# Moving row-reversed filter copies out of the head of a spectral-filter + FFN kernel, with a reordered table build

## Chip, cores, metric

One core of a Trainium2 chip. The metric is device time in microseconds (us). In the lines of profiles PE is TensorE, PEld its weight loads, DVE VectorE, ACT ScalarE, POOL GpSimd, and SPq SyncE issuing DMAs; L12 is a line of that kernel, `a<-b` writes a from b, and a bracket or a second `<-` names what ended a wait.

## The reference, cut

```python
g = sigmoid((x * gate_w).sum(-1, keepdims=True))
a = irfft2(rfft2(x) * (w_r + 1j * w_i))                    # S = 2048, D = 576
b = (gelu(B_x @ w_gate) * (B_x @ w_up)) @ w_down           # F = 4608
out = g * a + (1 - g) * b
# outputs: out and its vjp for x, w_r, w_i, w_gate, w_up, w_down, gate_w; bf16 inputs
```

## The kernel before

A *head* makes Fourier tables by rotation and runs the forward FFT of x; its tiles are stored to DRAM (`scr_x`). Then comes the FFN: 18 groups of 256 columns, four steps each. Every step starts with the z matmuls (L341), which need the group's transposed weights `wdT`. The remaining FFTs and the elementwise "mid" stage of the filter run as side work between the FFN's matmuls. A last phase is pure matmul. What the change touches:

```python
# u2(t), second FFT stage of tile t: evacuate from PSUM, store at once on SyncE's queue (LD)
    V.tensor_copy(Vt[:], vps[:, :, :2 * HF])                 # L538
    ...                                                      # or ScalarE, L540, for some tiles
    LD.dma_start(dst[t], Vt[:])                              # L541
...
# weights of group g, on the same queue, in three parts after steps 0, 1, 2 of group g - 1
    LD.dma_start_transpose(wts[g][1][:, 4:5, :], ...)        # part 1, L241
    LD.dma_start_transpose(wtmp[0][:], B_w_down[fsl, 0:512]) #         L242
    LD.dma_start(wdT[LO, 4, :], wdT[HI, 4, :])               # part 2, L245
    ... LD.dma_start(wdT[r, 2*par:2*par+2, :], wtmp[0][...]) # four moves, L248
...
# row-reversed copies, DRAM to DRAM: 32 of 2 x 128 x 72 elements (36 KB, one row fewer in two), 2 small
def reversed_rows(eng, src, dst):
    s_, d_ = (a.rearrange("(m i) (h l) -> h i m l", i=T, h=2) for a in (src, dst))
    return [lambda i=i: eng.dma_start(d_[:, i], s_[:, T - i, ::-1]) for i in range(1, T)] + ...
...
# head
for t in range(T):
    x1[t]()                                   # first FFT stage
    ...
    if t % 3 == 0 and t + 3 < T:
        build_R(nc, tb, unit, t + 3)          # rotation tables of three tiles
    if t > 0:
        x2[t - 1]()                           # second FFT stage
tail_table()                                  # odd inverse table
for k, v in enumerate((A_w_r, A_w_i)):        # filter copies on GpSimd's queue, all in the head
    for move in reversed_rows(nc.gpsimd, v[:, HF:DF], wrev[k][:]):
        move()
...
# FFN step
def side_work():
    for _ in range(3):                        # products of the mid stage, on VectorE
        if side: side.pop(0)()
...
for _ in range(3):                            # reversed output copies, on SyncE's queue
    if moves: moves.pop(0)()
```

`unit` buffers (tables, FFT tiles, products) share one pool of 19 slots. In the built program SyncE's queue is in order, and its DMAs use eight semaphores in turn, so each waits for the one eight places ahead of it.

Of the kernel before, what the change touches and what calls it, by code (L numbers as in the profile page):

```python
# [11 lines left out]
BF16 = mybir.dt.bfloat16  # L12
# [7 lines left out]
S, D, DF = 2048, 576, 289  # L20
P, T = 128, 16
# [19 lines left out]
HF = 145  # L41
# [60 lines left out]
def run_late(tb):  # L102
    while tb.late:
        tb.late.pop(0)()
# [32 lines left out]
def build_R(nc, tb, unit, t0):  # L137

    V = nc.vector
    n = min(3, T - t0)  # L140
    step = 2.0 * math.pi / S * EPS_SCALE
    X = unit([n, P], I32, name="XR")
    C = unit([n, P], I32, name="CR")
    for t in range(n):
        V.tensor_scalar(X[:, t, :], tb.krow[:], tb.scol[:, t0 + t:t0 + t + 1], None, op0=ALU.mult)
    V.tensor_scalar(C[:], X[:], float(S // 4), None, op0=ALU.add)
    V.tensor_single_scalar(X[:], X[:], S - 1, op=ALU.bitwise_and)
    V.tensor_single_scalar(C[:], C[:], S - 1, op=ALU.bitwise_and)
    o = unit([n, 3, P], name="Rt")

    for v, (ang, b, sc) in enumerate(((C, tb.pi, -step), (X, tb.npi, step), (X, tb.pi, -step))):
        tb.late.append(lambda v=v, ang=ang, b=b, sc=sc: nc.scalar.activation(o[:, :, v, :], ang[:], ACT.Sin, bias=b[:], scale=sc))
    tb.Rt += [o[:, t] for t in range(n)]
# [32 lines left out]
def kernel(  # L186
# [4 lines left out]
    nc = tc.nc  # L191
    LD = nc.sync
# [6 lines left out]
    unit = Unit(ctx.enter_context(tc.tile_pool(name="unit", bufs=NUNIT, side="right")))  # L199
# [12 lines left out]
    wrev, orev = ([dram.tile([S, DF - HF], BF16, name=f"{n}{k}") for k in range(2)] for n in ("wrev", "orev"))  # L212
# [40 lines left out]
    tb = iotas(nc, res, unit)  # L253
# [20 lines left out]
    pz = ps1.enter_context(tc.tile_pool(name="pz", bufs=1, space=PSUM))  # L274
# [16 lines left out]
    def headps():  # L291
        hctr[0] += 1
        pool, tag = ((pg, "pg"), (ph, "xy"), (pz, "z"), (ph, "xy"))[hctr[0] % 4]
        return pool, tag
# [90 lines left out]
    stores, moves = [], []  # L385
# [159 lines left out]
    def tail_table():  # L545

        n = HF - P
        nc.gpsimd.memset(tb.At2[:], 0.0)
        pool, tag = headps()
        tp_ = pool.tile([P, 2, 1024], BF16, tag=tag, name="tp")  # L550
        for c in range(2):
            nc.tensor.transpose(tp_[:, c, 0:P], tb.Dt[2][:, c, 0:P], ident[:])
            nc.tensor.transpose(tp_[0:n, c, 256:256 + P], tb.Dt[2][:, c, P:HF], ident[:])
            nc.tensor.transpose(tp_[:, c, 512:512 + 32], tb.Dt[3][0:32, c, 0:P], ident[0:32, 0:32])
            nc.tensor.transpose(tp_[0:n, c, 768:768 + 32], tb.Dt[3][0:32, c, P:HF], ident[0:32, 0:32])
        V.tensor_copy(tb.Oi[:, :, 0:P], tp_[:, :, 0:P])
        V.tensor_copy(tb.Oi[:, :, P:HF], tp_[:, :, 512:512 + n])
        ot = unit([2, HF], name="ot")
        V.tensor_copy(ot[0:n, :, 0:P], tp_[0:n, :, 256:256 + P])
        V.tensor_copy(ot[0:n, :, P:HF], tp_[0:n, :, 768:768 + n])  # L560
        for i in range(2):
            LD.dma_start(tb.At2[i * NL:i * NL + n, i, :, 0:HF], tb.Dt[1][0:n])
            LD.dma_start(tb.At2[i * NL + n:(i + 1) * NL, i, :, HF:2 * HF], ot[0:n])
# [17 lines left out]
    def tiles_of(t):  # L581
        return t[:].rearrange("(m i) l -> m i l", i=T)

    def reversed_rows(eng, src, dst):

        s_, d_ = (a.rearrange("(m i) (h l) -> h i m l", i=T, h=2) for a in (src, dst))
        return [lambda i=i: eng.dma_start(d_[:, i], s_[:, T - i, ::-1]) for i in range(1, T)] + \
            [lambda: eng.dma_start(d_[:, 0, 1:P], s_[:, 0, P - 1:0:-1]), lambda: eng.dma_start(dst[0:1], src[0:1])]

    a_dv = a_scr[:].rearrange("(m i) d -> m i d", i=T)  # L590
    dxa_dv = dxa_scr[:].rearrange("(m i) d -> m i d", i=T)
# [1 line left out]
    def mid_units():  # L593
# [36 lines left out]
        def products(p):  # L630
            X, G, W = st[p, "x"], st[p, "g"], st[p, "w"]
            i0 = 2 * p

            def halve(t):
                e = t[:].rearrange("p i c l -> p (i c) l")[:, :, 0:DF:DF - 1]
                V.tensor_scalar(e, e, 0.5, None, op0=ALU.mult)

            def bc(ap):
                return ap.unsqueeze(2).to_broadcast([P, 2, 2, DF])

            def mul(key, a, b):
                def f():
                    st[p, key] = unit([2, 2, DF], name=key)
                    V.tensor_tensor(st[p, key][:], a[:], bc(b), op=ALU.mult)
                return f

            def comb(k1, k2, conj):
                def f():
                    m1, m2 = st[p, k1], st[p, k2]
                    V.tensor_tensor(m1[:, :, 0, :], m1[:, :, 0, :], m2[:, :, 1, :], op=(ALU.add if conj else ALU.subtract))  # L650
                    V.tensor_tensor(m1[:, :, 1, :], m1[:, :, 1, :], m2[:, :, 0, :], op=(ALU.subtract if conj else ALU.add))
                return f

            def fold(key):

                def f():
                    m = st[p, key]
                    q = unit([2, 2, 2, HF], name="q" + key)
                    for e, op in enumerate((ALU.add, ALU.subtract)):
                        V.tensor_tensor(q[:, :, :, e, 0:HF - 1], m[:, :, :, 0:HF - 1], m[:, :, :, DF - 1:HF - 1:-1], op=op)  # L660
                    V.tensor_copy(q[:, :, :, :, HF - 1], m[:, :, :, HF - 1:HF].to_broadcast([P, 2, 2, 2]))
                    st[p, key + "_q"] = q
                return f

            def out_dw():
                o = st[p, "o1"]
                nc.gpsimd.tensor_scalar(o[:, :, 1, HF:DF], o[:, :, 1, HF:DF], -1.0, None, op0=ALU.mult)

                def store():
                    for k, v in enumerate((o2v, o3v)):  # L670
                        LD.dma_start(v[:, i0:i0 + 2, 0:HF], o[:, :, k, 0:HF])
                        LD.dma_start(tiles_of(orev[k])[:, i0:i0 + 2, :], o[:, :, k, HF:DF])
                    if p == T // 2 - 1:
                        for k, v in enumerate((out_2, out_3)):
                            moves.extend(reversed_rows(LD, orev[k][:], v[:, HF:DF]))
                stores.append(store)
            return [
                lambda: halve(G),
                mul("m1", X, W[:, 0]), mul("m2", X, W[:, 1]), comb("m1", "m2", False),
                lambda: (halve(st[p, "m1"]), fold("m1")()),  # L680
                mul("n1", G, W[:, 0]), mul("n2", G, W[:, 1]), lambda: (comb("n1", "n2", True)(), fold("n1")()),
                mul("o1", G, X[:, :, 0, :]), mul("o2", G, X[:, :, 1, :]), comb("o1", "o2", True),
                out_dw,
            ]
# [24 lines left out]
        out = [first] + [gap] * 3  # L709
# [92 lines left out]
    x1, x2 = fwd_units(xT, scr_x, None, ps=head_tile)  # L802
    build_R(nc, tb, unit, 0)
    run_late(tb)
    for t in range(T):
        x1[t]()
        if t % 4 == 2 and t < 14:
            tchunk(xn, xT, t + 2)
        if t >= 9 and t % 2 == 1:
            tchunk(dB, dOT, 2 * (t - 9))  # L810
        if t % 3 == 0 and t + 3 < T:
            build_R(nc, tb, unit, t + 3)
        if tb.late:
            tb.late.pop(0)()
        if t > 0:
            x2[t - 1]()
    build_B(nc, tb, unit, res)
    run_late(tb)
    tail_table()
    for k, v in enumerate((A_w_r, A_w_i)):  # L820
        for move in reversed_rows(nc.gpsimd, v[:, HF:DF], wrev[k][:]):
            move()
    x2[T - 1]()
    gate()

    fg = zipped(*fwd_units(dOT, scr_g, gs32))
    ia, pa = inv_units(scr_p1, a_dv, SD2)
    ib, pb = inv_units(scr_p2, dxa_dv, 1.0)
    mid = mid_units()
    fft = fg + [gap] * 5 + mid[:-2] + pa + mid[-2:] + [gap] * 2 + ia[:-4] + pb + ia[-4:] + ib  # L830

    fft_pos = [0]

# [49 lines left out]
    for g in range(NG):  # L883
# [3 lines left out]
        for m in range(NPR):  # L887
            pr = g * NPR + m
# [3 lines left out]
            hs = [h for u in pend[m] for h in u] if pend else []  # L892

            def side_work():
                for _ in range(3):
                    if side:
                        side.pop(0)()
            if g == 0 and m > 0:
                fft_next()
            z, xy_full = H_mm(g, m)  # L900
# [31 lines left out]
            else:  # L932
                jobs = [(0, sig0)] * bool(carry) + carry + [(1.7, second)] + [(0, sig0)] * (not carry) + hs
                us = sum(j[0] for j in jobs)
                at, k, late = 0.0, 1, [sig1]
# [18 lines left out]
                LD.dma_start(gwb[:], gate_w.partition_broadcast(P))  # L954
            if (g, m) in ((0, 3), (1, 0)):
                scale_dB(T // 2)
            for _ in range(3):
                if moves:
                    moves.pop(0)()
            if done[0] == n_slots or (pr >= wgT_from and pr % 2 == 0 and len(wgT_all) < 20):  # L960
                load_wgT()
                if done[0] == n_slots:
                    load_wgT()
# [232 lines left out]
```

## Time and profile before

| | median us | profiled span | mean granted clock | first z matmul |
|---|---|---|---|---|
| before (4 runs, 1489.52 to 1492.24) | 1490.91 | 1494.7 | 0.979 | 87.10 |

TensorE is the bound. Of the 80 us in which it idles, most lie ahead of the first z matmul: 29.2 in one wait. From there on an untouched group takes 52.0 us in the stretch that matters later (its z matmuls start at 394.58, 446.58, 498.63, 550.63). A start of a group's first z matmul is therefore a milestone that can be compared between kernels; I use that as a ledger below. The prediction shows the lines.

### The profile page before, as it was taken

To read this page: it belongs to the slowest core of one execution; us is meant where nothing else is said; L and a number is where in the kernel's file an instruction comes from. 1 tells how busy PE (TensorE), PEld (TensorE's weight loads), DVE (VectorE), ACT (ScalarE), POOL (GpSimd) and SP (SyncE) were. 2 spreads that over 40 slices of the span, in tenths; PEclk is the share of its full clock that TensorE was granted. 3 is DMA by queue.
4 is the path that set the end of the run, shared out by engine and by line. 5 is a ranking of instruction groups with operands and counts; after the bars stand their busy time and mean duration, and the time that the engine had idled before them with its cause. 6 is when DMAs were issued, how large, how long until landed. Compare 5 with 4: busy or idle time off the path is not lost.

```text
span 1494.7 us, 30032 instructions
## 1 busy us (share of the span) xinstructions
PE 1414.5 (95%) x11500; PEld 1050.8 (70%) x11586; DVE 887.8 (59%) x2356; ACT 697.2 (47%) x1380; POOL 172.1 (12%) x258
## 2 busy tenths in 40 slices
PE   4388999999999999998999999999999999999997
PEld 3255767767776776776677777777877777777775
DVE  6269777988898889867677777775000461212200
ACT  3267766666667767666667667664000000000000
POOL 6500011111111111111010010010000110000000
PEclk8699999999999999999999999999999999999998
DMA  9925454455565555446556546665999998878773
GB/s 167 75 76 132 118 147 128 122 136 129 137 155 128 132 141 135 114 103 144 139 133 160 143 127 154 161 143 138 274 199 194 209 213 159 167 158 170 153 150 67
DMA packets 550712, 217.87 MB, mean 146 GB/s; under 512 B 375368, under 2 KB 540424, under 8 KB 550568
## 3 DMA queue, kind: packets, MB, share of 16 engines
q1 hardware_dynamic: 537800, 194.03, 59.4%
q0 software_dynamic: 10960, 20.91, 6.0%
q8 instruction: 90, 1.47, 0.5%
q10 hardware_dynamic: 1808, 1.02, 0.2%
q14 instruction: 54, 0.44, 0.1%
HBM read 43.28 MB, written 96.22 MB: 93 GB/s over the span
## 4 chain that ended last, share of the span: by engine, by line
PE 77%; DVE 2%; issue 1%; DMA 0%; SPq 0%; ACT 0%; DVEq 0%
PE acc L1043 28%; PE wps L464 14%; PE xy L353 12%; PE wps L447 8%; PE z L341 7%; PE wps L477 2%; PE xy L348 2%; PE z L344 1%; PE pf L745 1%; PE pf L772 1%; PE pf L774 1%; DMA pin<-scr 0%; PE pf L695 0%; PE pf L696 0%; PE pf L698 0%
## 5 line engine op out<-in xcount | busy, mean ns | idle before, releaser
L1043 PEld LDWEIGHTS <-pin 128*128 128x128 bf16 x3456 | 338.0, 98 | 86.5 <-DMA pin<-scr 1.4
L353 PE MATMUL xy<-wgu,xT 128*128 128x512 bf16 x1066 | 257.9, 380 | 10.1 <-issue 8.3
L464 PEld LDWEIGHTS <-xn 128*128 128x128 bf16 x2304 | 225.1, 98 | 31.3 <-issue 0.2
L353 PEld LDWEIGHTS <-xT 128*128 128x128 bf16 x1152 | 106.9, 98 | 139.0 <-issue 31.8
L366 ACT ACTIVATE da<-z,omg 128x256 bf16<-128x256 f32 x288 | 113.3, 474 | 126.6 <-PE z L344 123.2
L1060 ACT COPY bo<-acc 128x288 f32<-128x288 f32 x32 | 12.8, 399 | 309.3 <-PE acc L1043 284.7
L447 PE MATMUL wps<-dB,A 128*128 128x288 bf16 x1152 | 152.7, 286 | 0.0
L341 PE MATMUL z<-wdT,dOT 128*128 128x256 bf16 x1152 | 141.1, 277 | 7.0 <-DMA wdT<-wtmp 4.4
L1043 PE MATMUL acc<-wd_all,pin 128*128 128x288 bf16 x1152 | 142.8, 286 | 1.1 <-DMA pin<-scr 1.1
L1043 PE MATMUL acc<-wgT,pin 128*128 128x288 bf16 x1152 | 143.6, 286 | 0.0
L1043 PE MATMUL acc<-wuT,pin 128*128 128x288 bf16 x1152 | 143.6, 286 | 0.0
L447 PEld LDWEIGHTS <-A 128*128 128x128 bf16 x1152 | 112.6, 98 | 34.9
L464 PE MATMUL wps<-dHg,xn 128*128 128x256 bf16 x1152 | 133.1, 273 | 0.0
L464 PE MATMUL wps<-dHu,xn 128*128 128x256 bf16 x1152 | 132.0, 273 | 0.0
L341 PEld LDWEIGHTS <-dOT 128*128 128x128 bf16 x1152 | 112.5, 99 | 26.2 <-issue 6.5
L1120 DVE SCALAR_TENSOR_TENSOR f32t<-gwf,dlog,b16t 128x576 f32<-128x576 f32 x16 | 13.1, 817 | 179.2 <-DMA b16t<-dxa_scr 179.2
L372 ACT ACTIVATE q<-xy 128x512 bf16<-128x512 f32 x144 | 86.1, 598 | 66.0 <-PE xy L353 62.3
L396 ACT ACTIVATE om<-s 128x512 bf16<-128x512 bf16 x144 | 92.0, 639 | 23.7 <-DVE s L380 23.6
L470 POOL DMA_DIRECT2D out_dram<-dw x67 | 48.9, 730 | 440.7 <-ACT dw L425 290.6
L397 ACT ACTIVATE s<-s 128x512 bf16<-128x512 bf16 x144 | 90.7, 630 | 4.6
L378 ACT CAST hu<-xy 128x512 bf16<-128x512 f32 x144 | 87.0, 604 | 0.0
L379 DVE TENSOR_SCALAR s<-q 128x512 bf16<-128x512 bf16 x144 | 41.9, 291 | 73.2 <-ACT q L372 72.5
(213 smaller groups left out, 1846.8 us busy)
## 6 DMA issues: line engine op xcount, KB each, us to landing
scr<-A SPq DMA_DIRECT2D x144, 128.0 KB
scr<-dHg SPq DMA_DIRECT2D x144, 128.0 KB
scr<-dHu SPq DMA_DIRECT2D x144, 128.0 KB
out_dram<-dw POOLq DMA_DIRECT2D x67, 128.0 KB, 2.9
wd_all<-in_B_w_down_dram SPq DMA_DIRECT2D x3, 1728.0 KB
out_dram<-dwd POOLq DMA_DIRECT2D x34, 144.0 KB, 3.2
wgu<-in_B_w_gate_dram SPq DMA_DIRECT2D x18, 256.0 KB
wgu<-in_B_w_up_dram SPq DMA_DIRECT2D x18, 256.0 KB
```

The source lines that it names most:

```text
L341: nc.tensor.matmul(zo(t), lhsT=dOT[:, ci, t, :], rhs=wdT[:, ci, :], start=(t % 4 < 2 and ci == 0), stop=False)
L353: nc.tensor.matmul(xy[k][:, t % 2, :], lhsT=xT[:, ci, t, :], rhs=wgu[:, ci, :], start=False, stop=(ci == 3))
L366: nc.scalar.activation(da[:, tt, :], z[:, tt, k, :], ACT.Copy, scale=omg32[:, t:t + 1])
L372: nc.scalar.activation(q[:], xy[:, :, 0:FG], ACT.Square)
L378: nc.scalar.copy(hu[:], xy[:, :, FG:2 * FG])
L379: V.tensor_scalar(s[:], q[:], A_GELU, 1.0, op0=ALU.mult, op1=ALU.add)
L396: nc.scalar.activation(om[:], s[:], ACT.Sigmoid, scale=-2.0 * C_GELU)
L397: nc.scalar.activation(s[:], s[:], ACT.Sigmoid, scale=2.0 * C_GELU)
L447: nc.tensor.matmul(wps[:, :288], lhsT=tl(0, t)[:, fch * P:(fch + 1) * P], rhs=dB[:, t, h * 288:(h + 1) * 288], start=(t == 0), stop=(t == ...
L464: nc.tensor.matmul(wps[:, cc, :], lhsT=xn[:, t, (c0 + cc) * P:(c0 + cc + 1) * P], rhs=tl(k, t), start=(t == 0), stop=(t == T - 1))
L470: wst[0].dma_start(ov[:, c0:c0 + TPB, fsl], dw[:])
L1043: nc.tensor.matmul(acc[:, :288], lhsT=src[:, r, :], rhs=w_of(r)[:, h * 288:(h + 1) * 288], start=(first and r == 0), stop=(last and r == F ...
```

## The change

Its intent: take the 34 filter copies out of the head, where they share the DMA engines with the loads and stores that hold the FFT up; give the table build and the second FFT stage a tile of slack; spread the copies over the first two groups; make the output copies as soon as each row pair is done.

```diff
@@ tail_table
-        pool, tag = headps()
-        tp_ = pool.tile([P, 2, 1024], BF16, tag=tag, name="tp")
+        tp_ = pz.tile([P, 2, 1024], BF16, tag="z", name="tp")
@@ reversed_rows: the same copies, all on SyncE's queue, for the tiles asked for
-    def reversed_rows(eng, src, dst):
+    def reversed_rows(src, dst, tiles):
...
@@ out_dw, store
-                    if p == T // 2 - 1:
-                        for k, v in enumerate((out_2, out_3)):
-                            moves.extend(reversed_rows(LD, orev[k][:], v[:, HF:DF]))
+                        moves.extend(reversed_rows(orev[k][:], (out_2, out_3)[k][:, HF:DF], [(T - i) % T for i in (i0, i0 + 1)]))
@@ head
-        if t % 3 == 0 and t + 3 < T:
-            build_R(nc, tb, unit, t + 3)
+        if t % 3 == 1 and t + 2 < T:
+            build_R(nc, tb, unit, t + 2)
...
-        if t > 0:
-            x2[t - 1]()
+        if t > 1:
+            x2[t - 2]()
+    x2[T - 2]()
...
-    tail_table()
-    for k, v in enumerate((A_w_r, A_w_i)):
-        for move in reversed_rows(nc.gpsimd, v[:, HF:DF], wrev[k][:]):
-            move()
+    for i in range(T):
+        for k, v in enumerate((A_w_r, A_w_i)):
+            moves.extend(reversed_rows(v[:, HF:DF], wrev[k][:], [i]))
...
-    fft = fg + [gap] * 5 + mid[:-2] + ...
+    fft = fg + [tail_table] + [gap] * 4 + mid[:-2] + ...
@@ FFN step
-                for _ in range(3):
+                for _ in range(4):
                     if side:
...
-            for _ in range(3):
+            for _ in range(5 if pr < 8 else 2):
                 if moves:
                     moves.pop(0)()
+            assert pr != 8 or not moves
```

More of the change, by code (lines that the diff above doesn't have):

```diff
@@ L582, in tiles_of @@
         return t[:].rearrange("(m i) l -> m i l", i=T)
-    def reversed_rows(eng, src, dst):
+    def reversed_rows(src, dst, tiles):
         s_, d_ = (a.rearrange("(m i) (h l) -> h i m l", i=T, h=2) for a in (src, dst))
-        return [lambda i=i: eng.dma_start(d_[:, i], s_[:, T - i, ::-1]) for i in range(1, T)] + \
-            [lambda: eng.dma_start(d_[:, 0, 1:P], s_[:, 0, P - 1:0:-1]), lambda: eng.dma_start(dst[0:1], src[0:1])]
+        out = []
+        for i in tiles:
+            if i:
+                out.append(lambda i=i: LD.dma_start(d_[:, i], s_[:, T - i, ::-1]))
+            else:
+                out.append(lambda: LD.dma_start(d_[:, 0, 1:P], s_[:, 0, P - 1:0:-1]))
+                out.append(lambda: LD.dma_start(dst[0:1], src[0:1]))
+        return out
     a_dv = a_scr[:].rearrange("(m i) d -> m i d", i=T)
@@ L829 @@
     mid = mid_units()
-    fft = fg + [gap] * 5 + mid[:-2] + pa + mid[-2:] + [gap] * 2 + ia[:-4] + pb + ia[-4:] + ib
+    fft = fg + [tail_table] + [gap] * 4 + mid[:-2] + pa + mid[-2:] + [gap] * 2 + ia[:-4] + pb + ia[-4:] + ib
     fft_pos = [0]
```

## The prediction

> **What bounds the kernel now.** I read the page first. TensorE is busy 95% of the span, and its row of 40 slices says where it is not: slices 1 to 3 (37 us each) hold nearly all the gap, and the granted clock falls there too.
>
> ```profile
> PE 1414.5 (95%) x11500; PEld 1050.8 (70%) x11586; DVE 887.8 (59%) x2356; ACT 697.2 (47%) x1380; POOL 172.1 (12%) x258
> ...
> PE   4388999999999999998999999999999999999997
> ...
> PEclk8699999999999999999999999999999999999998
> ```
>
> Idle TensorE time is 1494.7 - 1414.5 = 80 us. From 93 us on almost every microsecond is matmul, so a microsecond saved ahead of the first FFN matmul (87.10) is a microsecond of the total, unless something later makes TensorE wait anew. The waits of the first 140 us name the big one:
>
> ```profile
> PE fx L530 <- ACT Y L519: 35.7, 4, 29.2
> ...
> ACT Rt L152 <- DMA scr_x<-Vt: 28.1, 1, 28.1
> ```
>
> TensorE waits 29.2 us for a copy on ScalarE, which stands behind a rotation table (Rt), which waits for a *store* of a forward-FFT tile (Vt to scr_x). A table need not wait for a store in its data; both live in the same 19-slot pool, so it waits for the slot. The timeline of SyncE's queue tells why that store is late:
>
> ```profile
> 19.97 3.62 SPq L241 DMA_TRANSPOSE wdT<-in_B_w_down_dram  x1
> 23.64 4.16 SPq L242 DMA_TRANSPOSE wtmp<-in_B_w_down_dram  x1
> 34.24 0.50 SPq L245 DMA_DIRECT2D wdT<-wdT  x1
> 39.25 6.83 SPq L248 DMA_DIRECT2D wdT<-wtmp  x4
> 46.18 37.20 SPq L541 DMA_DIRECT2D scr_x<-Vt  x15
> ```
>
> The first Vt was ready at 16.4, but its store is behind the loads of the first weights, whose last moves wait for the DMA transposes (6.4 and 4.4 us of waiting on that queue). It is issued at 46.18 and lands about 55.5. Meanwhile GpSimd's queue runs the row-reversed filter copies (wrev), from 8 to 70 us:
>
> ```profile
> 8.45 7.81 POOL L587 DMA_DIRECT2D wrev<-in_A_w_r_dram  x7
> ...
> 68.86 1.61 POOL L588 DMA_DIRECT2D wrev<-in_A_w_i_dram  x2 [1.45 <-issue]
> ```
>
> In 25 to 45 us the software queue holds 10 to 75% of the 16 engines' time while the whole core moves only 32 to 56 GB/s. The transposes, issued at 20 to 28, have landed at 39. In a later group the same transposes, issued at 530.1 and 531.3, have landed before 537.5, when the moves behind them go out without waiting.
>
> **What the Trainium skill says.** "DMA: Bandwidth & Descriptors", section "Issuing engines are not separate DMA queues": DMAs of all issuing engines run on the same 16 DMA engines and interleave. The trace agrees: GpSimd's copies slow SyncE's transposes. The same page, "Why a DMA increments its semaphore by 16 and not by 1", says that a hardware-issued DMA uses the largest count up to 16 that divides the slowest dimension of both patterns. A reversed copy is 2 x 128 x 72, so 2 engines. The trace agrees: while the existing reversed output copies run alone on SyncE's queue (about 711 to 713) the DMA share is 0.1 to 0.2 at 16 to 28 GB/s. "TensorE: Matmul & The Clock Gate", "What's actually happening", says the array falls to half clock after an idle window of about 3.4 us. The trace agrees: granted clock 0.50 in 40 to 60 us, and 0.75 in 710 to 720 after a wait of 3.81.
>
> **The change part by part.**
>
> *Removed from the head:* 34 wrev DMAs on GpSimd. Without them I estimate the weights: the x and grad loads end near 17 as before; the 1280 rows of the two first weight slices took about 8 us beside the copies and take 4 to 5 later in the trace, so 21 to 22; the transposes need 5 to 6 us as at 530, so 27; the four moves 2.65 us as later in the trace, so about 30; the first scr_x store lands near 32.
>
> *Rotation angles one tile later, second FFT stage two tiles behind:* in the built program the first slot wait on a scr_x store is now on VectorE's angles for tiles 9 to 11, made after tile 7, and ScalarE's first on a store is the copy of tile 9 instead of the table before tile 7. Tile 7 ran at 28.7, so VectorE gets there at about 28 and waits to 32. So the TensorE gap shrinks from 29.2 to about 4.5: **-24.5 us**. The two later waits of ScalarE for scr_x stores (3.9 us together) should mostly go, as the queue is no longer behind: **-3**. Without the long idle, the half-clock restart after 58.8 is mostly saved: **-1.5**.
>
> *The odd table:* 8 small transposes, 1.07 us of TensorE at 82.0 to 83.1, move into the FFN loop (slot 33, about step 8). TensorE is the bound there too: **0**.
>
> *Added to SyncE's queue:* the same 34 copies, five after each of the first seven FFN steps. What one costs there is to be read off the output copies of the same shape:
>
> ```profile
> 696.57 3.93 SPq L587 DMA_DIRECT2D out_dram<-orev  x3
> 700.61 2.09 SPq L412 DMA_DIRECT2D scr<-A  x1
> ```
>
> Three copies and the store behind them hold the queue 6.1 us; an undisturbed store takes 0.45, so 1.9 us a copy, 9.5 for five. A step of the first group lasts 10 us (first z matmuls at 87.10, 98.68, 108.65, 118.88, then 128.84), and the queue's own work fills most of it: its gaps are about 3.5 us a step. So it falls behind. The deadline is the transposed weights of group 1: in the trace their last moves go out just in time.
>
> ```profile
> 124.05 2.64 SPq L248 DMA_DIRECT2D wdT<-wtmp  x4
> ...
> 128.84 1.91 PE L341 MATMUL z<-wdT,dOT 128*128 128x256 bf16 x16 [0.83 <-ACT Y L521]
> ```
>
> Counting from the first z: weight loads done at 20; five copies, 29.5; stores, 33; transposes, 35.7; five copies, 45; stores, 49; moves, 52; landed 54. Wanted at 41.7: a wait of up to 12 us, or 6 if a copy costs 1.3. For group 2 the same count gives about 205 - 87 = 118 against 99.8 + 12: up to 6 more, or none at 1.3. I put this at **+13** with the half-clock restart.
>
> *Output copies two a step as each pair of rows is done, not three a step at the end:* in the trace before, they cause exactly such a wait:
>
> ```profile
> 706.42 0.55 SPq L245 DMA_DIRECT2D wdT<-wdT  x1
> 707.02 2.63 SPq L248 DMA_DIRECT2D wdT<-wtmp  x4
> ...
> 709.90 0.58 PE L341 MATMUL z<-wdT,dOT 128*128 128x256 bf16 x2 [3.81 <-DMA wdT<-wtmp]
> ```
>
> 3.81 + 0.63 us, and the next 10 us run at clock 0.75, about 2 us more. At two a step, four in about 3.6 steps, the queue is held under 4 us, and 8 to 10 us lie between moves and use in most groups of that stretch: **-6**. Four side products a call instead of three only move VectorE work earlier: 0.
>
> Sum: -24.5 - 3 - 1.5 + 13 - 6 = -22. **Predicted: 1469 us.**
>
> **The rivals.** *The copies hide on SyncE's queue.* They begin at 28 GB/s, 1.3 us each, and the queue has gaps; then the loss is about 6 us and the time 1462. For it: only two DMA engines are used. Against: three of them already made TensorE wait at 709.9.
>
> *The congestion is worse.* Five in a row settle at 16 GB/s, 2.2 us each; the lag reaches group 2, and FFT tiles (whose slots also wait for stores on this queue, with about ten slots free) hold up ScalarE: 20 to 24 us lost, time 1476 to 1480.
>
> *The loads, not the copies, hold the store.* 4.7 MB of x and grad must pass first in any case, and GpSimd's copies carry only 1.2 MB. Then the first store lands near 40, the gap is still 12 us, and the time is 1476. Against: the transposes took 2 to 3 times as long as in a later group, while engines were busy and bytes few.
>
> *The reordering alone would do it.* One tile of slack is about 2 us of TensorE work; it cannot absorb 28 us, so I give it 2 to 4 us of the gain.
>
> **Range and chances.** The head should give 24 to 33 us, the output copies 2 to 7, the queue takes 5 to 22. If the ends don't all meet, 1455 to 1482 holds it 8 times in 10. Over 2% faster means under 1461.3: it needs a cheap queue and a full head gain, 0.28. Slower by over 2% would need the queue to lose over 50 us: 0.02. Within 2%: 0.70.
>
> **What would show it.** Right: the first z matmul at 52 to 58 instead of 87; first scr_x store issued near 30; a TensorE wait of some 5 to 12 us on wdT at the start of group 1, about 42 us later, and perhaps on the next; no wdT wait near 700. Wrong: SyncE's transposes still landing near 39 without the copies (head), or the four moves for group 1 issued within 40 us of the first z (queue), or a new wait on slots in the first group.

## More of the kernel before

PSUM is the memory in which TensorE's results land here and which VectorE or ScalarE empties.

## The result

| | median us | profiled span | clock | first z matmul |
|---|---|---|---|---|
| before | 1490.91 | 1494.7 | 0.979 | 87.10 |
| after (4 runs, 1494.00 to 1496.41) | 1494.28 | 1492.2 | 0.985 | 49.44 |

Ratio 1.0026 (1.0008 to 1.0043): the same within 2%, and outside the predicted range. A ratio here is the mean time of one kernel's runs over that of the other's runs of the same rounds, so it is not quite the ratio of the medians quoted.

The page of the changed kernel, TensorE and its granted clock in 40 slices of 37 us:

```profile
PE   7959599899999999999999999999999999999997
...
PEclk9979799999999999999999999999999999999999
```

The hole at slices 1 to 3 is gone, but slices 3 and 5 now hold two new ones, and the clock dips with each (granted clock 0.57 in 90 to 105 us, around the first, and 0.87 in the 15 us after it). The waits of TensorE in the first 200 us name both, and what is left of the old stall:

```profile
PE z L341 <- DMA wdT<-wtmp: 31.3, 4, 15.9
...
PE tp L303 <- DVE Vt L538: 3.0, 1, 3.0
```

(Columns: total us, number of waits, longest.) The 29.2 us wait of the head has become 3.0, and TensorE waits 31.3 us at the starts of groups 1 and 2 for weights. First the head, on SyncE's queue of the changed kernel:

```profile
16.29 1.22 SPq L241 DMA_TRANSPOSE wdT<-in_B_w_down_dram  x1
...
21.56 0.49 SPq L245 DMA_DIRECT2D wdT<-wdT  x1
22.26 2.65 SPq L248 DMA_DIRECT2D wdT<-wtmp  x4
```

With no copies beside them the transposes have landed at 21.6 instead of 34 to 39, the four moves take 2.65 us instead of 6.83, and the first FFT store is issued at 25.00 instead of 46.18. Then the same queue, and TensorE behind it, between steps 2 and 4 of the FFN:

```profile
81.98 1.28 SPq L242 DMA_TRANSPOSE wtmp<-in_B_w_down_dram  x1
83.31 0.67 SPq L589 DMA_DIRECT2D wrev<-in_A_w_i_dram  x1
...
87.28 2.84 SPq L589 DMA_DIRECT2D wrev<-in_A_w_r_dram  x1
90.17 2.65 SPq L589 DMA_DIRECT2D wrev<-in_A_w_i_dram  x1
92.92 2.56 SPq L541 DMA_DIRECT2D scr_g<-Vt  x1
...
100.40 2.65 SPq L248 DMA_DIRECT2D wdT<-wtmp  x4
...
103.29 0.59 PE L341 MATMUL z<-wdT,dOT 128*128 128x256 bf16 x2 [14.14 <-DMA wdT<-wtmp]
```

Five copies and the store that waits behind the last of them hold the queue from 83.31 to 95.48, 12.2 us. The first two go out quickly, then each holds the queue for 2.2 to 2.8 us. The DMA eight places ahead is not what holds them: that of the third copy had landed by 80.92. By the trace's semaphore updates the five land about 2.7 us apart (87.98, 90.70, 93.40, 96.12, 98.82), and from the third on an issue ends 0.6 to 0.7 us before the copy two places ahead has landed. What limits the queue to about two of them at a time, no run shows. The four moves for group 1 leave at 100.40, 51 us after the first z matmul, and TensorE has waited 14.14 us. What the DMA engines did meanwhile (DMA view of the changed kernel, 85 to 96 us; busy share in tenths, then the total):

```profile
DMA  1111111111111111100011111111001111111111
...
DMA packets 1194, 0.17 MB, mean 16 GB/s; under 512 B 1190, under 2 KB 1194, under 8 KB 1194
```

A tenth of 16 engines is about two. The queue is full, the core's DMA engines are nearly idle.

A third loss is small and repeats: TensorE's waits from 300 to 1050 us, of before and then of the changed kernel.

```profile
PE pf L695 <- ACT da L366: 2.8, 1, 2.8
```
```profile
PE pf L698 <- ACT da L366: 7.1, 5, 1.5
```

One of these, on VectorE, ScalarE and TensorE; before:

```profile
407.73 0.29 DVE L379 TENSOR_SCALAR s<-q 128x512 bf16<-128x512 bf16 x1
...
409.78 1.55 ACT L366 ACTIVATE da<-z,omg 128x256 bf16<-128x256 f32 x4
```

and after:

```profile
408.36 0.84 DVE L665 TENSOR_TENSOR qn<-n 128x576 bf16<-128x576 bf16 x2
...
409.18 0.28 DVE L379 TENSOR_SCALAR s<-q 128x512 bf16<-128x512 bf16 x1
...
410.03 0.63 ACT L396 ACTIVATE om<-s 128x512 bf16<-128x512 bf16 x1 [1.40 <-DVE s L380]
...
411.23 1.55 ACT L366 ACTIVATE da<-z,omg 128x256 bf16<-128x256 f32 x4
412.83 0.28 PE L698 MATMUL pf<-qn,Rt 128*128 128x290 bf16 x1 [1.42 <-ACT da L366]
```

The fourth side product puts another fold (qn) on VectorE ahead of the GELU's `s`. ScalarE waits 1.40 us for `s`; behind that in its order stands `da`, which empties the z tile in PSUM; and the next FFT matmul, which needs that PSUM, waits 1.42 us. The five waits (7.1 us) lie in groups 6 to 10, one in each; in groups 4 and 5 a z matmul waits 4.5 and 1.2 us behind ScalarE's `Vt` instead (before: the 2.8 above, in group 4).

**The ledger.** Lead over the kernel before (us, positive is earlier) at the first z matmul of a group, from the traces; the last four columns are experiments told below:

| group | after | e1_side3 | e2_forward | e6_pool_paced | e7_again |
|---|---|---|---|---|---|
| 0 | 37.7 | 40.0 | 39.1 | 37.9 | 39.7 |
| 1 | 25.5 | 27.7 | 37.9 | 27.4 | 40.9 |
| 2 | 8.5 | 9.7 | 36.8 | 27.9 | 40.9 |
| 3 | 4.3 | 6.2 | 35.7 | 26.8 | 39.9 |
| 11 | -7.7 | 6.6 | 21.5 | 13.1 | 37.2 |
| 13 | -0.8 | 13.5 | 28.3 | 19.9 | 44.0 |
| 17 | -0.9 | 13.5 | 28.3 | 19.9 | 44.0 |

For the changed kernel: head +37.7, groups 0 to 2 -33.4, groups 3 to 10 -12.0 (about 1.6 a group from group 5 on), groups 11 and 12 +6.8, and nothing after. The sum is -0.9; the medians differ by 3.4 and the two profiled spans by 2.5 the other way, which is the size of the scatter between runs.

### The profile page after: what moved, and what is told of

It is laid out like the page before. It is cut to its first block, busy times and chain, and to the rows that moved or that the text cites. A ratio compares the mean times of both kernels' runs of the same rounds, so it can differ in the third digit from the quotient of the medians.

```text
span 1492.2 us, 30025 instructions
## 1 busy us (share of the span) xinstructions
PE 1413.8 (95%) x11500; PEld 1050.0 (70%) x11586; DVE 886.3 (59%) x2356; ACT 695.5 (47%) x1380; POOL 136.1 (9%) x224
## 4 chain that ended last, share of the span: by engine, by line
PE 57%; issue 0%; DVE 0%; ACT 0%; DVEq 0%
PE acc L1047 28%; PE wps L464 8%; PE xy L353 7%; PE wps L447 5%; PE z L341 4%; PE wps L477 1%; PE pf L748 1%; PE xy L348 1%; PE z L344 1%; PE pf L775 1%; PE pf L777 1%; PE pf L761 0%; ACT da L366 0%; DVE n L649 0%; PE pf L698 0%
## 5 line engine op out<-in xcount | busy, mean ns | idle before, releaser
L341 PE MATMUL z<-wdT,dOT 128*128 128x256 bf16 x1152 | 142.5, 278 | 37.6 <-DMA wdT<-wtmp 31.3
L1124 DVE SCALAR_TENSOR_TENSOR f32t<-gwf,dlog,b16t 128x576 f32<-128x576 f32 x16 | 13.1, 818 | 176.7 <-DMA b16t<-dxa_scr 176.7
```

The source lines that it names most:

```text
L341: nc.tensor.matmul(zo(t), lhsT=dOT[:, ci, t, :], rhs=wdT[:, ci, :], start=(t % 4 < 2 and ci == 0), stop=False)
```

## The experiments

Theory T: the 37.7 us of the head are real and lost again, two thirds or more to the copies on SyncE's queue, 12 us to the fourth side product. Rivals: the copies only need DMA time somewhere, so any place costs the same (R1); the late losses also come from the copies, or from the head's new order (R2). Twelve runs of eleven kernels were made, in three batches, each on one chip with its own runs of before (medians 1493.31, 1490.47 and 1493.93). All passed the tolerance.

**e1_side3**: the changed kernel, three side products a call.

```diff
-                for _ in range(4):
+                for _ in range(3):
```

> The changed kernel with three side products a call instead of four; all else as changed. My theory: the 12 us that the changed kernel's lead loses between groups 3 and 10 come from four side products ahead of the gelu work on VectorE, which delays ScalarE's da and with it TensorE. Then this run is about 11 us faster than the changed kernel (1483), its lead over the kernel before stays level from group 3 to 10, and the two waits on wdT at groups 1 and 2 are as in the changed kernel (14.8 and 15.9 us). Rival: that loss comes from the output copies two a step; then nothing changes (1494).

Measured 1483.09, ratio to before 0.9916 (0.9881 to 0.9951). In the ledger the loss of groups 3 to 10 is gone (6.2 to 6.6), the waits on `da` from 300 to 1050 us fall from 7.1 to 0.4, and all else is as after. So side products cost 12 us, and R2 falls for that part.

**e2_forward**: the changed kernel, with 30 of the 34 filter copies not reversed. Wrong; the tolerance does not see it.

```diff
-                out.append(lambda i=i: LD.dma_start(d_[:, i], s_[:, T - i, ::-1]))
+                if "wrev" in str(kind):      # 128 x 144 instead of 2 x 128 x 72
+                    out.append(lambda i=i: LD.dma_start(tiles_of2(dst)[:, i], tiles_of2(src)[:, T - i]))
+                else:
...
```

> Wrong result on purpose (filter gradients and outputs): 30 of the 34 filter copies keep the row order, so that their pattern is 128 x 144 and can use 16 DMA engines; same number, bytes and place in SyncE's queue. Theory: what clogs the queue is that a reversed copy runs on 2 engines (2.4 us each in a burst of five); here a copy costs about 0.5 us, the waits on wdT at groups 1 and 2 go (under 2 us together), and the time is about 1460. Rival: copies between two places in HBM are slow in themselves, or the number of DMAs in the queue is; then waits of over 10 us stay and the time is over 1475.

Measured 1466.16, ratio 0.98 (0.976 to 0.9841). The same copies on SyncE's queue by duration, changed kernel and then e2_forward (count, then min/median/max in ns, first and last start):

```profile
L589 SPq DMA_DIRECT2D wrev<-in_A_w_i_dram x15: 607/2593/3101, 83.3 to 182.3; - x15
```
```profile
L593 SPq DMA_DIRECT2D wrev<-in_A_w_i_dram x15: 502/596/597, 80.0 to 140.5; - x15
```

The bytes, the queue and the program order are the same, and of the waits on wdT 0.6 us is left. So it is the shape of the copies that holds the queue. The edit changes two things of the shape, the engines (2 to 16) and the length of a row (144 to 288 bytes); no run separates the two. The traces do show the engines: after each of the 32 copies of the changed kernel that are reversed in this way the copy's semaphore gets 3 updates, one just after the issue and two as data land (for the copy issued at 83.31: 84.43, then 86.88 and 87.98), and after each of the 30 that e2_forward changed it gets 16.

**e3_pool_issue**: the changed kernel, copies issued by GpSimd at the same program places.

```diff
-                out.append(lambda i=i: LD.dma_start(d_[:, i], s_[:, T - i, ::-1]))
+                out.append(lambda i=i: eng.dma_start(d_[:, i], s_[:, T - i, ::-1]))   # eng = GpSimd
```

> The changed kernel with the 34 filter copies issued by GpSimd instead of SyncE, at the same places in the program (GpSimd may run ahead of them). Theory: the loss at groups 1 and 2 is SyncE's in-order queue; with the copies off it the waits on wdT go and the time is about 1460 to 1465. Rival: it is the load on the DMA engines that the copies share with the transposes; then the transposes are late as in the head of the kernel before, waits on wdT of over 10 us stay, and the time is over 1480.

A miss as an experiment: measured 1492.98, ratio 0.998 (0.9943 to 1.0017). GpSimd had nothing to wait for, ran ahead of the FFN and issued the copies from 7.4 us on, in the head. What it did show: with them there, the old wait is back at 29.2 us although the new order is in, and there is no wait on wdT. Since its program differs from the changed kernel's in the issuing engine alone, and its run in when the copies went out, that ties the head's wait to the copies' being there.

**e5_no_rot**: the changed kernel with the old order of table build and second FFT stage.

```diff
-        if t % 3 == 1 and t + 2 < T:
-            build_R(nc, tb, unit, t + 2)
+        if t % 3 == 0 and t + 3 < T:
+            build_R(nc, tb, unit, t + 3)      # and x2[t - 1]() at t > 0
```

> The changed kernel with the rotation angles and the second FFT stage at their old places. Theory: the head's gain of 37.7 us is the removal of the filter copies from the head; the reordering is worth 2 to 6 us of it, so the first z matmul starts at 52 to 56 instead of 49.4 and the time is 1496 to 1500. Rival: the reordering carries a large part; then the first z matmul starts later than 62.

Measured 1497.20, ratio 1.0005 (0.9968 to 1.0041); its first z matmul leads by 38.5 us, as much as with the new order. So the order carries none of it (48.58, before the expected 52 to 56): the gain comes with the copies' absence. (The odd table, 1.07 us of TensorE, has left the head here too.)

**e6_pool_paced**: e3_pool_issue mended. A tiny GpSimd copy that reads the step's A tile stands ahead of each batch, so that GpSimd keeps pace.

```diff
+            if moves and pr < 8:
+                nc.gpsimd.tensor_copy(pace[:], kept[g][-1][0][:, 0, 0:1])
             for _ in range(5 if pr < 8 else 2):
```

> As e3 (filter copies issued by GpSimd in the FFN loop), but ahead of each batch of five GpSimd copies one column of that step's activation tile, so that it cannot run ahead into the head as it did in e3 (there the old 29 us wait came back). Theory, SyncE's in-order queue is what is lost at groups 1 and 2: first z matmul near 49, no wait on wdT over 4 us, lead at group 2 still over 33 us, time 1460 to 1466. Rival, the load on the shared DMA engines: the transposes land late, waits on wdT of over 8 us together stay, time over 1472.

Measured 1475.21, ratio 0.9888 (0.9855 to 0.9922). TensorE's one wait on wdT, and the moves it waits for:

```profile
PE z L342 <- DMA wdT<-wtmp: 10.8, 1, 10.8
```
```profile
93.10 6.43 SPq L248 DMA_DIRECT2D wdT<-wtmp  x4
```

Off SyncE's queue, the copies no longer delay group 2 (its 15.9 us are gone), but group 1 still waits 10.8, and the four moves take 6.43 us, much as in the head before (6.83). The expectation failed, and its rival's lines (over 8 us, over 1472) were met. The trace points to the shared engines: between 80 and 92 us SyncE's stores take 0.9 to 2.0 us each to issue, where e7_again's mostly take 0.4 to 0.5 in the same steps, and in 78 to 99 us the packets of GpSimd's queue take 42.4% of the engines' time. So the place in the in-order queue costs some 22 us (lead 26.8 against 4.3 at group 3) and sharing the engines about 11. R1 is half right for this form.

**e7_side3_two**: the changed kernel with three side products, and two copies a step from the start instead of five. Each copy still precedes the load that reads it: 20 are issued before the first such load, which needs 6.

```diff
-                for _ in range(4):
+                for _ in range(3):
...
-            for _ in range(5 if pr < 8 else 2):
+            for _ in range(2):
...
-            assert pr != 8 or not moves
```

> Changed kernel with three side products a call and two filter copies a step (SyncE) instead of five, over 17 steps; each copy still precedes the load that reads it. Theory: two copies cost the queue about 4 us a step against gaps of about 3.5, so the lag at the deadline of group 1 is under 5 us: waits on wdT of 0 to 5 us at groups 1 and 2 instead of 31, mid stage level as in e1, time 1450 to 1458, faster than both kernels by over 2%. Rival, any copy in that queue costs its full 2.4 us: the waits stay over 12 us together, time over 1463.

Measured 1450.55, ratio 0.9723 (0.969 to 0.9757), and in the third batch as **e7_again** 1449.95, ratio 0.9707 (0.9688 to 0.9726): faster than both kernels.

> e7 once more, on the same chip as e4, e10 and e11: 1449 to 1453, 2.5 to 3% faster than the kernel before, no wait on wdT.

The page of e7_again, TensorE and its clock; then, from its timeline, the moves and the matmul of group 1:

```profile
PE   7989999899999999999999999999999999999997
...
PEclk9999999999999999999999999999999999999999
```
```profile
83.40 2.66 SPq L248 DMA_DIRECT2D wdT<-wtmp  x4
...
87.90 1.91 PE L341 MATMUL z<-wdT,dOT 128*128 128x256 bf16 x16 [0.83 <-ACT Y L521]
```

No wait on wdT in either group. The same 34 copies, same queue, same shape, in portions of two fit between the steps' stores, and the moves leave at 83.40. Added up over the timeline, issuing the copies takes SyncE 31.3 us, where fives take 59.3, since only the first two of a batch go out quickly; the store behind a batch takes about 2 us or more in most steps of both. R1 falls. A remaining loss of 2.7 us between groups 3 and 11 stays as it is; its waits from 200 us on are behind ScalarE (3.0 for `da`, 1.8 for an FFT tile).

**e8_side3_pool**: e6_pool_paced with three side products (its edit and that of e1_side3).

> e6 with three side products a call. If both theories hold the gains add up: e6 less 11 us, 1449 to 1455. If the mid-stage loss depended on when the filter copies land, e8 differs from e6 by less than 5.

Measured 1459.73, ratio 0.9786 (0.9746 to 0.9827), 15.5 below e6_pool_paced of the same batch; the wait on wdT at group 1 stays at 10.1. The gains add up, though the time is above the expected 1449 to 1455, which had been set before e6_pool_paced came out higher than expected.

**e9_before_side4**: the kernel before with four side products.

```diff
-                for _ in range(3):
+                for _ in range(4):
```

> The kernel before with four side products a call instead of three and nothing else. Theory: the side products alone cost 10 to 13 us between groups 3 and 10, time 1501 to 1504. Rival: they cost only together with the rest of the change; time within 3 us of the kernel before.

Measured 1504.26, ratio 1.0081 (1.0046 to 1.0116). With none of the copies moved it loses 13.8 us; in its ledger the lead goes from +4.2 at group 3 (a head that happened to be shorter) to -8.3 at group 11. The cost belongs to the side products alone. That this head, the same program as before's, had its first z matmul 4.2 us earlier also tells how far a head with the copies in it scatters from run to run: its long wait was 26.3 us instead of 29.2.

**e4_rot_only**: the kernel before with only the new order (the diff of e5_no_rot, reversed).

> The kernel before with the rotation angles a tile later and the second FFT stage two tiles behind, nothing else; the filter copies stay in the head. Prediction on record: the reordering alone gives 2 to 4 us. e3, where the copies ran ahead into the head, had its first z matmul at 78.6 instead of 87.1, so I now expect 6 to 9: the head's long wait stays (25 us or more), the first z matmul starts near 79, and the time is 1482 to 1486. Rival: that was the table moved out of the head; then under 3 us.

A miss: measured 1495.07, ratio 1.0005 (0.9979 to 1.0031), and the first z matmul at 86.71, 0.4 us early and not 6 to 9. The long wait only changes its name:

```profile
PE tp L303 <- DVE Vt L538: 31.6, 1, 31.6
```

**e10_two_no_rot**: e7_side3_two with the old order.

> e7 (three side products, two filter copies a step) with the rotation angles at their old place. e5 lost nothing in the head by it (first z matmul at 48.6), so: within 3 us of e7 (1449 to 1454). If the reordering matters here it is 5 us or more slower.

Measured 1450.87, ratio 0.9713 (0.9694 to 0.9731), 0.9 us above e7_again beside it, with overlapping intervals. The new order is worth nothing that these runs can resolve, with the copies in the head or without.

**e11_two_side4**: two copies a step, four side products.

> The changed kernel with two filter copies a step, side products left at four. If the two losses are independent this is e7 plus the 11 to 14 us that four side products cost in e1 and e9: 1461 to 1465, with no wait on wdT at groups 1 and 2. If they interact, it is more than 5 us off that.

Measured 1459.42, ratio 0.9773 (0.9754 to 0.9791), 9.5 above e7_again of the same batch (a little under the expected 1461 to 1465), with no wait on wdT. The fourth product costs here 9.6 us net between groups 3 and 11 (12.3 lost against 2.7).

## Why the prediction was wrong

By its own terms, in us gained:

| term | predicted | ledger of after |
|---|---|---|
| head | +29 | +37.7 |
| copies on SyncE's queue | -13 | -33.4 |
| fourth side product | 0 | -12.0 |
| output copies | +6 | +6.8 |
| sum | +22 | -0.9 |

Two terms failed: the queue's, mis-sized by 20 us, and the fourth side product's, forecast as nothing. That the time stayed within 2% of before, to which the prediction gave 0.70, is luck: 44.5 us of gains met 45.4 us of losses. (Its 2% line of 1461.3 should read 1461.1.)

**Head: right in kind, too small.** The wait shrank by 26.2 (predicted 24.5), and the first store left at 25.00, not near 30. The other 11.5 lie outside the gap: tile 7's first-stage matmuls run at 22.87 instead of 28.72, so 5.9 ahead of it, which the prediction did not book, and 5.6 after it, for which it had 4.5. It is the absence of the copies (e5_no_rot: 38.5), not the order (e4_rot_only: a lead of 0.4, less than the scatter of 4 us). The rival "the loads, not the copies, hold the store" is dead.

**Order: "I give it 2 to 4 us of the gain" failed**; it is 0 within about 1 us (e10_two_no_rot; e4_rot_only agrees). That one tile of slack cannot absorb the store's delay was right.

**Queue: the mechanism was right, the term mis-sized by 20 us.** The step that failed is "I put this at +13". Its own count had group 1's weights landing 54 us after the first z matmul, and TensorE went on 53.9 after it, a wait of 14.8 against "up to 12", longer because TensorE was ready a little earlier. For group 2 the count gave 118; the weights came near 129, because a copy in a burst cost 2.4 (12.2 us for five) and not 1.9. There the wait was 15.9 us, and another 4.2 went within that group, where the granted clock was 0.77 over 179 to 190 us. The rival "the congestion is worse" described this, with 2.2 us a copy and a lag that reaches group 2, but its 20 to 24 us were still too few. Even the dear case of the prediction's count, 12 and 6 added up to 18 us, falls 15 short, and +13 lies between it and a cheap case (1.3 us a copy) that did not come. The lag of the in-order queue was carried from group to group, so what a copy was under-priced by was paid again at the second deadline.

**Side products: "only move VectorE work earlier: 0" failed outright.** The prediction gives no working for it. VectorE's 59% is a mean over the whole span; in a group of that stretch (394.58 to 446.58 us before) VectorE is busy 45.5 of 52.0 us, and the place in its order decides: the added fold holds up ScalarE's `da`, which empties PSUM, and so TensorE. Four pairs of kernels that differ in the number of side products alone show it. By the ledger the fourth product costs between groups 3 and 11: 12.4 us (after against e1_side3), 12.5 (e9_before_side4 against before), 9.6 (e11_two_side4 against e7_again) and 14.0 (e6_pool_paced against e8_side3_pool).

**Output copies: right, though not tried alone.** The 3.81 us wait near 709 is gone (changed kernel):

```profile
713.59 1.91 PE L341 MATMUL z<-wdT,dOT 128*128 128x256 bf16 x16
```

Every kernel with the new output copies in the ledger gains 6.8 or 6.9 between groups 11 and 13; the two kernels with the old ones (e4_rot_only, e9_before_side4) gain nothing there.

**Odd table: 0.** No wait names it; it was not tried alone.

Open: why e3_pool_issue, with its copies in the head, still had its first z matmul 8.5 us early (78.6). The order does not explain it; the scatter of such a head, 4.2 us between before and e9_before_side4, may be half of it. Open, too, is which DMA holds group 1 in e6_pool_paced: most on SyncE's queue are slow there, not one.

## What to carry to other kernels

Cost a DMA on an in-order queue by its pattern as well as its bytes, and schedule it in portions that the queue's slack per step can swallow: here five at once lost 33 us, two at once none, for the same work. Carry the lag of such a queue from deadline to deadline and add up the waits of all (here 14.8 and 15.9 us). Before calling elementwise work on an engine with spare time free, look for what stands behind it there: here it was the work that empties PSUM, behind an engine with a busy share of 59% over the span.

## What the Trainium skill lacked or had wrong

- "DMA: Bandwidth & Descriptors", section "Issuing engines are not separate DMA queues", says that starting DMAs on several engines only saves the sequencer's issue time, usually small. Here it was not small: a copy in a burst took SyncE 2.2 to 2.8 us to issue, and with the same copies moved from SyncE's to GpSimd's queue the lead at group 3 was 26.8 instead of 4.3 us (e6_pool_paced), since a full in-order queue holds up what stands behind. The other half of the section agrees: on the shared engines the copies still made group 1 wait 10.8 us.
- The same page, "Why a DMA increments its semaphore by 16 and not by 1", gives the count of engines but not what a copy on few engines costs its issuing queue. Here a 36 KB copy of outer size 2 took 2.59 us (median) in the queue at a DMA share of 0.1, one of outer size 128 with twice the row length 0.60 us.
- No page that I found tells how side work ahead of a PSUM evacuation reaches TensorE; here it cost 1.4 us a group in groups 6 to 10 of the changed kernel, and 9.6 to 14.0 us in all.
